# Two preparations of batch 2 issued ahead of theta of batch 1 instead of inside the attention of batch 1

## The chip, the core and the metric

The kernel runs on one core of a Trainium2 chip. The metric is the device time of one execution in microseconds (us), as the median of several runs. Engines: PE (TensorE) multiplies matrices, DVE (VectorE) and ACT (ScalarE) work elementwise, POOL (GpSimd) and SP (SyncE) mostly issue DMAs here. Each engine takes its instructions in order; semaphores make one wait for another.

## The reference

Two stages follow each other: a local attention with a few global keys, and a token-mixing layer with a phase. Inputs are q, k, v of 4 batches, 8 heads, 768 tokens, 64 channels, and four weights; the output is 4 x 768 x 512 in float32.

```python
scores = scale * q @ k.T - slope_h * dist        # kept: key < 8, or 0 <= query - key < 96
a = softmax(scores over the kept keys)
x = concat over heads of (a @ v)                 # 768 x 512
theta = x @ w_theta
y = w_tok_r @ (x * cos(theta)) + w_tok_i @ (x * sin(theta))
u = x + y
out = u + relu(u @ w_ch)
```

## The kernel before, in words

**Tiling.** 768 tokens are 6 tiles of 128. Heads go in 4 pairs, since two heads of 64 channels fill the 128 partitions. For a pair, `prep` (L249) copies q and k from the load buffer into qkn with the heads of a token side by side (`prep_copy`, L241, two DVE copies at L246), transposes qkn on PE (L261, 6 for q and 6 for k), copies the two results out as qT (DVE, L265) and kT (ACT, L267), and builds kG, the keys with the 8 global ones put in front of tiles 1 to 4 (`kglob`, L229, DVE at L235 and L237). `prep` of pair p also makes the copies of pair p+1. `score_mms` (L303) computes the kept blocks of scores of a pair in three chunks (L319) into a large PSUM buffer (`big`, 2 buffers of two banks); `score_exp` (L325) takes exp on ACT (L329) and multiplies by a table of biases on DVE (L338, L341). `values` (L362) multiplies by v (L381, also into a large PSUM buffer) and divides into x_sb (L386, L388). `xtrans` (L390) makes xT, the transpose of x_sb of a pair: in batch 1 by a DMA transpose issued by SP for pairs 0 to 2 (L392), by PE (L399) and ACT (L400) for pair 3.

**Mixing.** `theta` (L405) multiplies xT by w_theta (L422), over the four pairs dc = 0 to 3 in this order; `sines` (L427) takes cos and sin on ACT (L432, tile cs) and multiplies by x on DVE (L436, tile zri). `mix` (L441) does the token mixing of one output tile in three groups of four matmuls (L447) and adds x into u (L452). `utrans` (L456) transposes u (by PE at L465 for batch 0, by SP's DMA at L461 later), `chan` (L468) multiplies by w_ch (L475), adds on DVE (tile o_sb, L480) and stores by SP (L482). There are four small PSUM buffers (tile ps), which the transposes, the mix and chan share.

**Order of the work.** Batches overlap: while the mix of batch b runs on PE, the attention of batch b+1 is woven in. `weave` (L531) issues a list of main steps (mix, chan) and places side steps (the attention) between them by their weights. In batch 0 the four preps of batch 1 are side steps as well, ahead of the attention. Two preps of batch 2, for pairs 0 and 1, are in the list `ahead` (L652); `attention_steps` (L502) puts the first behind the fifth block of scores (L520) and the second behind the last one (L525), with a weight of 1536 each. Pairs 2 and 3 of batch 2 are prepared inside batch 2's own attention (L507, L519). Between two batches stands a boundary, the list `order` (L654): one remaining chan, the first four parts of theta, one more of the remaining steps (in batch 1 the utrans of the last tile of batch 0), the other two parts of theta, the remaining chans. In batch 1 `load_behind` (L496) stands ahead of it: a POOL copy (L497) reads a value of xT of pair 3, and behind it POOL issues the loads of the second half of batch 3's q and k (L82, 8 of 96 KB) and of its v (L88). The first half of batch 3's q and k is issued at the end of the weave of batch 0 (L679).

The part up to the middle of batch 0 is ordered by hand. From there a scheduler orders each engine's instructions, by the order of issue in the program and its own estimates; `behind` (L201) and `issue_after` keep given instructions behind an anchor. In `prep` the qkn copies stay behind the latest u (anchor "dve") and the transposes behind the latest mix matmul (anchor "pe").

POOL's loads run in the DMA queue q0 (software_dynamic), SP's transposes and stores in q1 (hardware_dynamic); both use the same 16 DMA engines.

Of the kernel before, what the change touches and what calls it, by code (L numbers as in the profile page):

```python
# [16 lines left out]
def kernel(  # L17
# [19 lines left out]
    NP = H // 2  # L37
# [18 lines left out]
    def ps_small(shape, dtype):  # L56
        return small.tile(shape, dtype, name="ps", tag="ps")
# [5 lines left out]
    def alloc_qk(b):  # L63
        loads[b] = [ld.tile([T, 2, H, NT, D], BF, name="qk"), None]
# [136 lines left out]
    def behind(eng):  # L201

        return tc.issue_after(anchor[eng]) if eng in anchor else nullcontext()
# [25 lines left out]
    def kglob(b, p, t0=0, t1=NT - 2, copy=nc.vector.tensor_copy):  # L229
        kT = qkT[(b, p)][1]  # L230
        if t0 == 0:
            qkT[(b, p)][2] = att.tile([T, NT - 2, T], BF, name="kG", bufs=6)
        kG = qkT[(b, p)][2][:, t0:t1]
        with behind("zri" if p else "dve") if b == B - 1 else nullcontext():
            copy(  # L235
                out=kG, in_=kT[:, (t0 + 1) * T:(t1 + 1) * T].rearrange("p (t n) -> p t n", t=t1 - t0))
            copy(out=kG[:, :, 0:NG], in_=kT[:, None, 0:NG].to_broadcast([T, t1 - t0, NG]))  # L237
# [3 lines left out]
    def prep_copy(b, p):  # L241
        qk = loads[b][0]
        qkn = qkns[b, p] = att.tile([T, NT, 2, 2, D], BF, name="qkn", bufs=2)
        with behind("dve"):
            for i_ in range(2):
                nc.vector.tensor_copy(  # L246
                    out=qkn[:, :, i_].rearrange("p t h d -> p h t d"), in_=qk[:, i_, 2 * p:2 * p + 2])

    def prep(b, p):  # L249
        if p == 0 or (b, p) == (2, NP // 2):  # L250
            prep_copy(b, p)
        if p + 1 < NP and (b, p) != (2, NP // 2 - 1):
            prep_copy(b, p + 1)
        qkn = qkns[b, p]
        qT = att.tile([T, S], BF, name="qT", bufs=6)
        kT = att.tile([T, S], BF, name="kT", bufs=6)
        for i_, dst in ((0, qT), (1, kT)):
            ps = ps_small([T, NT, T], BF)
            with behind("pe"):
                for t_ in range(NT):  # L260
                    nc.tensor.transpose(ps[:, t_, :], qkn[:, t_, i_].rearrange("p h d -> p (h d)"), ident)  # L261
            dst = dst.rearrange("p (n t) -> p n t", t=NT)
            src = ps.rearrange("p t n -> p n t")
            if i_ == 0:
                nc.vector.tensor_copy(out=dst, in_=src)  # L265
            else:
                nc.scalar.copy(out=dst, in_=src)  # L267

        qkT[(b, p)] = [qT, kT, None]
        kglob(b, p)  # L270

    def prep_dma(b, p):
        qk = loads[b][0]
        qkT[(b, p)] = [None, None, None]
        for i_ in (1, 0):
            to = qkT[(b, p)][i_] = att.tile([T, S], BF, name=("qT", "kT")[i_], bufs=6)
            with behind("sp"):
                nc.sync.dma_start_transpose(
                    out=to.rearrange("p (t s) -> p t s", t=NT),
                    in_=qk[:, i_, 2 * p:2 * p + 2].rearrange("p h t d -> p (h t d)"))  # L280
# [124 lines left out]
    def theta(b, c, j):  # L405
        last0 = [(j_, NC - 1) for j_ in range(2)]
        part = {0: [(0, dc) for dc in range(NC - 1)],
                1: [(1, dc) for dc in range(NC - 1)] + last0,
                2: [(j_, dc) for dc in range(NC - 1) for j_ in range(2)],
                3: last0,  # L410
                4: [(j_, dc) for dc in range(NC - 2) for j_ in range(2)],
                5: [(j_, NC - 2) for j_ in range(2)]}[j]
        if c == 0 and j in (0, 2, 4):
            zri[b] = moe.tile([T, 2, NT, DM], BF, name="zri", tag="zri", bufs=1)
        xT, xb = xT_sb[b], x_sb[b]
        last = c == NT // 2 - 1
        if j in (0, 2, 4):
            pss["th", c] = [ps_small([T, DM], FP) for _ in range(2)] if last else ps_big()
        pb = pss["th", c]
        st = lambda j_: slice((2 * c + j_) * T, (2 * c + j_ + 1) * T)  # L420
        for j_, dc in part:
            nc.tensor.matmul(pb[j_] if last else pb[:, j_, :], lhsT=xT[:, dc, st(j_)],  # L422
                             rhs=w_theta_bf[:, dc, :], start=(dc == 0), stop=(dc == NC - 1))
        if j == 1:
            sines(b, c)
# [15 lines left out]
    def mix(b, tt, g):  # L441
        if g == 0:
            pss["mix", tt] = ps_small([T, DM], FP)
        ps = pss["mix", tt]
        for wi in range(2):
            for st in (2 * g, 2 * g + 1):
                anchor["pe"] = nc.tensor.matmul(  # L447
                    ps, lhsT=w_tokT[wi][:, st, tt * T:(tt + 1) * T], rhs=zri[b][:, wi, st, :],
                    start=(st == 0 and wi == 0), stop=(st == NT - 1 and wi == 1)).ins
        if g == NT // 2 - 1:  # L450
            u_sb[b, tt] = moe.tile([T, DM], BF, name="u", bufs=6)
            anchor["dve"] = nc.vector.tensor_add(  # L452
                u_sb[b, tt].rearrange("p (g d) -> p g d", g=NP), x_sb[b][:, :, tt, :],
                ps.rearrange("p (g d) -> p g d", g=NP)).ins

    def utrans(b, tt):  # L456
        u = u_sb[b, tt]
        uT = moe.tile([T, NC, T], BF, name="uT", bufs=5)
        uTs[(b, tt)] = uT
        if (b or b) and (b, tt) != (B - 1, NT - 1):  # L460
            anchor["sp"] = nc.sync.dma_start_transpose(out=uT, in_=u).ins  # L461
            return
        ps = ps_small([T, NC, T], BF)
        for dc in range(NC):
            nc.tensor.transpose(ps[:, dc, :], u[:, dc * T:(dc + 1) * T], ident)  # L465
        nc.scalar.copy(out=uT, in_=ps)  # L466
# [22 lines left out]
    def load_all_v(b):  # L489
        alloc_v(b)  # L490
        load_v(b, 0, 8)
# [4 lines left out]
    def load_behind(b, tile):  # L496
        g = nc.gpsimd.tensor_copy(out=gate, in_=tile).ins  # L497
        with tc.issue_after(g):
            load_qk_tokens(b, H // 2, H // 2)
            load_all_v(b)  # L500
# [105 lines left out]
    p = NP - 1  # L606
# [39 lines left out]
    rest = []  # L646
    for b in range(B):
        nxt = b + 1 if b + 1 < B else None
        lag = 3
        th = [lambda c=c, j=j: theta(b, c, j) for c in range(NT // 2) for j in range(2)]  # L650
        pre = [lambda p=p: prep(1, p) for p in range(NP)] if b == 0 else []
        ahead = [[lambda p=p: prep(2, p) for p in range(NP // 2)], [lambda p=p: prep_dma(3, p) for p in range(1)],  # L652
                 [], []][b]
        order = rest[:1] + th[:4] + rest[1:2] + th[4:] + rest[2:] if b else []  # L654
        if b == 2:
            order[:0] = [lambda p=p: prep_dma(3, p) for p in range(1, NP)]
        if b == 1:
            order.insert(0, lambda: load_behind(3, xT_sb[1][0:1, NC - 1, 0:1]))
        for f in order:
            f()  # L660
        main = []
        for tt in range(0 if b else 2, NT):
            for g in range(NT // 2):
                if (b, tt) != (B - 1, NT - 1):
                    main.append((2048, lambda tt=tt, g=g: mix(b, tt, g)))
                if b == 0 and g == 1 and 4 <= tt + 2 < NT:
                    main.append((1536, lambda tt=tt: trans_w(tt + 2)))
                if tt >= lag and g == 0 and (b, tt) != (B - 1, NT - 1):
                    main.append((2048, lambda tt=tt: chan(b, tt - lag)))
                if b == 0 and g == 1:  # L670
                    main.append((512, lambda tt=tt: utrans(b, tt - 1)))
                if (b, tt, g) == (0, 2, 0):
                    main.append((512, lambda: utrans(0, 0)))
            if b and (b, tt) != (B - 1, NT - 1):
                main.append((0, lambda tt=tt: utrans(b, tt)))
        side = [(1536, f) for f in pre]
        if b == 0:
            side[:0] = [(0, lambda: load_all_v(2))]
            side.append((0, lambda: (alloc_qk(3), load_qk_tokens(3, 0, H // 2))))  # L679
        side += attention_steps(nxt, ahead) if nxt else []  # L680
        weave(main, side, 0.1 if b == 0 else 0.0, 0.9)
        rest = [lambda tt=tt, b=b: chan(b, tt) for tt in range(NT - lag, NT)]
        if b == 0:
            rest.insert(1, lambda b=b: utrans(b, NT - 1))
# [44 lines left out]
```

## Time and profile before

| what | value |
|---|---|
| runs | 172.28, 172.26, 171.69 us; median 172.26 |
| profiled execution | span 170.0 us; no time beside the span is recorded for it |
| PE busy | 158.1 us (93%) |
| DVE, ACT, POOL busy | 125.9 (74%), 102.1 (60%), 37.6 us (22%) |
| granted TensorE clock | 1.000 |
| chain that ended last | PE 56%, DMA 19%, DVE 16%, ACT 6% |
| 48.60 to 66.20 us (17.60) | PE busy 16.28, DVE 17.59, ACT 13.06 |
| 66.20 to 70.70 us (4.50) | PE busy 3.57, DVE 4.47, ACT 1.29 |
| 70.70 to 105.20 us (34.50) | PE busy 33.99, DVE 26.92, ACT 22.41 |

The profile is one execution, with times in us from the start of the span. The chain that ended last is followed back from the last instruction: each step is what released the next. The timeline lists instructions in order of time, like ones merged ("x3"); a bracket gives the idle time of the engine before them and what ended it. Busy time of PE is pipelined: matmuls of 512 columns are listed with 0.38 us each and follow each other every 0.22 us. The attention of batch 1 lies in about 43 to 68 us, the boundary between batch 0's mix and batch 1's theta at about 66 to 71 us.

### The profile page before, as it was taken

What the parts mean: (1) busy time and instruction counts of PE and PEld (TensorE: products, weight loads), DVE (VectorE), ACT (ScalarE), POOL (GpSimd) and SP (SyncE); (2) the same over time, 40 slices, a digit from 0 to 9 for tenths busy, and PEclk for the clock granted to TensorE, in tenths of its full rate; (3) what the DMA queues carried; (4) which work ended last, traced back from release to release, by engine and by line L of the source; (5) the groups of instructions that cost most, each with busy time, mean ns of one, the idle gap of its engine ahead of it and who ended that gap; (6) DMA issues with size and microseconds to landing.
All of it is one profiled execution on the core that took longest, in us unless ns stands there. A gap on an engine that the chain in (4) does not pass through costs nothing.

```text
span 170.0 us, 3773 instructions
## 1 busy us (share of the span) xinstructions
PE 158.1 (93%) x1544; PEld 85.4 (50%) x1566; DVE 125.9 (74%) x267; ACT 102.1 (60%) x131; POOL 37.6 (22%) x45
## 2 busy tenths in 40 slices
PE   7679999999989899799999999999999999999991
PEld 2346765657645555345555464444554644444440
DVE  6748877699989999957998787788776847614432
ACT  4698898995596585399954561899257309400010
POOL 8976319005262110696000000000000000000000
PEclk9999999999999999999999999999999999999999
DMA  4999999999999999999996879688135472233335
GB/s 147 205 171 179 210 207 205 203 209 180 152 203 189 188 153 182 127 163 149 184 112 57 165 167 130 132 152 241 35 77 139 113 169 80 109 61 93 93 93 185
DMA packets 73488, 25.53 MB, mean 150 GB/s; under 512 B 61568, under 2 KB 70528, under 8 KB 73472
## 3 DMA queue, kind: packets, MB, share of 16 engines
q0 software_dynamic: 45680, 12.45, 77.1%
q1 hardware_dynamic: 27376, 12.33, 32.9%
q10 hardware_dynamic: 416, 0.52, 0.9%
q8 instruction: 12, 0.20, 0.5%
q14 instruction: 4, 0.03, 0.0%
HBM read 25.69 MB, written 6.29 MB: 188 GB/s over the span
## 4 chain that ended last, share of the span: by engine, by line
PE 56%; DMA 19%; DVE 16%; ACT 6%; issue 2%; DVEq 0%
PE ps L447 26%; DMA vn<-in_v_dram 14%; PE ps L475 9%; PE pb L422 6%; PE pb L319 4%; PE pb L381 3%; PE ps L422 3%; DMA xT<-x_sb 3%; DMA qk<-in_k_dram 3%; DVE x_sb L388 3%; DVE e L338 2%; ACT e L329 2%; PE ps L215 1%; ACT cs L432 1%; DVE e L341 1%
## 5 line engine op out<-in xcount | busy, mean ns | idle before, releaser
L447 PE MATMUL ps<-zri,w_tokT 128*128 128x512 bf16 x272 | 67.5, 380 | 1.1 <-issue 0.3
L329 ACT ACTIVATE e<-pb 128x1024 bf16<-128x1024 f32 (+1 forms) x48 | 43.4, 954 | 17.4 <-PE pb L319 17.0
L447 PEld LDWEIGHTS <-w_tokT 128*128 128x128 bf16 x288 | 25.9, 98 | 27.8 <-DVE w_tokT L183 0.6
L452 DVE TENSOR_TENSOR u<-x_sb,ps 128x512 bf16<-128x512 bf16 x24 | 16.3, 680 | 11.7 <-PE ps L447 11.6
L475 PE MATMUL ps<-w_ch_bf,uT 128*128 128x512 bf16 (+1 forms) x96 | 24.1, 371 | 0.2
L436 DVE TENSOR_TENSOR zri<-x_sb,cs 128x1024 bf16<-128x1024 bf16 (+1 forms) x30 | 16.6, 581 | 6.3 <-ACT cs L432 6.1
L480 DVE SCALAR_TENSOR_TENSOR o_sb<-ps,u 128x512 f32<-128x512 f32 (+1 forms) x25 | 16.4, 663 | 4.1 <-PE ps L475 4.1
L319 PE MATMUL pb<-qT,kT 64*128 64x128 bf16 x224 | 15.4, 219 | 2.2 <-DVE qT L226 1.2
L338 DVE TENSOR_TENSOR e<-e,etab 128x1024 bf16<-128x1024 bf16 (+1 forms) x24 | 14.8, 618 | 3.1 <-ACT e L329 3.0
L432 ACT ACTIVATE cs<-pb,halfpi 128x1024 bf16<-128x1024 f32 x8 | 8.9, 1116 | 12.5 <-PE pb L422 12.4
L422 PE MATMUL pb<-w_theta_bf,xT 128*128 128x512 bf16 x62 | 15.0, 379 | 1.1 <-DMA xT<-x_sb 0.9
L319 PEld LDWEIGHTS <-kT 64*128 64x128 bf16 x224 | 8.9, 94 | 13.2 <-issue 11.3
L466 ACT COPY uT<-ps 128x512 bf16<-128x512 bf16 x7 | 4.2, 594 | 18.3 <-PE ps L465 18.1
L381 PEld LDWEIGHTS <-e 128*128 128x128 bf16 x352 | 13.0, 97 | 4.3 <-issue 1.6
L422 PEld LDWEIGHTS <-xT 128*128 128x128 bf16 x96 | 9.1, 98 | 11.8 <-DMA xT<-x_sb 1.9
L475 PEld LDWEIGHTS <-uT 128*128 128x128 bf16 x100 | 9.1, 98 | 9.6 <-ACT uT L466 0.8
L88 POOL DMA_DIRECT2D vn<-in_v_dram x5 | 9.6, 1915 | 12.7 <-DVE qkn L246 10.4
L319 PE MATMUL pb<-qT,kG 64*128 64x128 bf16 x128 | 11.5, 216 | 0.3 <-DVE kG L237 0.2
L388 DVE TENSOR_TENSOR x_sb<-pb,rec 128x768 bf16<-128x768 f32 x12 | 11.4, 953 | 0.3
L381 PE MATMUL pb<-vn,e 128*128 128x65 bf16 x168 | 9.9, 193 | 0.7 <-DVE x_sb L388 0.3
L341 DVE TENSOR_TENSOR e<-e,etab 128x1024 bf16<-128x1024 bf16 x12 | 8.2, 687 | 2.4 <-ACT e L329 2.4
L267 ACT COPY kT<-ps 128x768 bf16<-128x768 bf16 x8 | 6.4, 798 | 4.6 <-PE ps L261 4.4
(81 smaller groups left out, 209.4 us busy)
## 6 DMA issues: line engine op xcount, KB each, us to landing
out_dram<-o_sb SPq DMA_DIRECT2D x23, 256.0 KB, 2.3
vn<-in_v_dram POOLq DMA_DIRECT2D x3, 768.0 KB, 22.5
qk<-in_q_dram POOLq DMA_DIRECT2D x2, 768.0 KB, 21.1
qk<-in_k_dram POOLq DMA_DIRECT2D x2, 768.0 KB, 24.2
w_nat<-in_moe_w_tok_r_dram POOLq DMA_DIRECT2D x3, 384.0 KB, 15.7
w_nat<-in_moe_w_tok_i_dram POOLq DMA_DIRECT2D x3, 384.0 KB, 15.2
vn<-in_v_dram POOLq DMA_DIRECT2D x2, 384.0 KB, 10.2
qk<-in_q_dram POOLq DMA_DIRECT2D x8, 96.0 KB, 8.6
```

Source lines behind the costliest of these rows:

```text
L319: nc.tensor.matmul(pb[:, hh, o:o + T], lhsT=lhsT, rhs=qT[R, (own, nxt)[part]], start=bool(b), stop=bool(b) or (jt == NT - 1 or (j == 1 and ...
L329: ins = nc.scalar.activation(e_c, pb[:, :, 0:n], AF.Exp, scale=scale).ins
L338: nc.vector.tensor_mul(e_c, e_c, tab[:, :, s0:s0 + n // T].rearrange("p a s n -> p a (s n)"))
L381: nc.tensor.matmul(po4[:, head - h0, it - i0], lhsT=l_, rhs=r_, start=(i_ == 0), stop=(i_ == len(mms) - 1))
L388: nc.vector.tensor_mul(xv, po4[:, :, :, 0:D], rec.to_broadcast([T, n, nt, D]))
L422: nc.tensor.matmul(pb[j_] if last else pb[:, j_, :], lhsT=xT[:, dc, st(j_)], rhs=w_theta_bf[:, dc, :], start=(dc == 0), stop=(dc == NC - 1))
L432: nc.scalar.activation(o, p_, AF.Sin, **bias)
L436: anchor["zri"] = nc.vector.tensor_mul(zri[b][:, i_, 2 * c + j_:2 * c + j_ + n, :].rearrange("p j (g d) -> p j g d", g=NP), xb[:, :, 2 * c ...
L447: anchor["pe"] = nc.tensor.matmul(ps, lhsT=w_tokT[wi][:, st, tt * T:(tt + 1) * T], rhs=zri[b][:, wi, st, :], start=(st == 0 and wi == 0), ...
L452: anchor["dve"] = nc.vector.tensor_add(u_sb[b, tt].rearrange("p (g d) -> p g d", g=NP), x_sb[b][:, :, tt, :], ps.rearrange("p (g d) -> p g ...
L475: nc.tensor.matmul(ps_c, lhsT=uT[:, dc, :], rhs=w_ch_bf[:, dc, i_ * n:(i_ + 1) * n], start=(dc == 0), stop=(dc == NC - 1))
L480: nc.vector.scalar_tensor_tensor(o_sb[:, cols], in0=ps_c, scalar=0.0, in1=u[:, cols], op0=ALU.max, op1=ALU.add)
```

## The change

The two preps leave the list of `attention_steps`, which for batch 1 has no preps any more, and stand in the boundary of batch 1 between the first chan and theta. The boundaries of batches 2 and 3 stay as they were. `weave` of batch 0 has two side steps of 1536 less, so the other side steps get slightly different places between the main steps.

```diff
-        ahead = [[lambda p=p: prep(2, p) for p in range(NP // 2)], [lambda p=p: prep_dma(3, p) for p in range(1)],
+        ahead = [[], [lambda p=p: prep_dma(3, p) for p in range(1)],
                  [], []][b]
-        order = rest[:1] + th[:4] + rest[1:2] + th[4:] + rest[2:] if b else []
+        pr = [lambda p=p: prep(2, p) for p in range(NP // 2)]
+        order = rest[:1] + pr + th[:4] + rest[1:2] + th[4:] + rest[2:] if b == 1 else rest[:1] + th[:4] + rest[1:2] + th[4:] + rest[2:] if b else []
```

On each engine the number of instructions stays the same. In the new order of PE the 24 transposes of the two preps (L261) stand in one block: behind the last mix of batch 0, the transposes of x_sb of pair 3 (L399), of u (L465) and a chan (L475), and ahead of all 16 matmuls of the first four parts of theta (L422); in the order before, the first two of these 16 stood ahead of L399. On DVE the four qkn copies stand behind the last u of batch 0, followed by an o_sb, the two qT and the kG copies, and the vG copies of batch 2; zri comes after them. On ACT the two kT copies stand between the copy of xT of pair 3 with a copy of uT, and the first cs. The orders of SP and of POOL are unchanged.

## The prediction

> **What bounds the kernel now.** I read the page first: the busy table gives PE 93% of the span, and the chain that ended last is PE for 56%. But the 40 slices show DVE as full as PE in slices 12 to 15 (about 48 to 66 us), and this is where the change works. So I read the chain in order of time. It runs on DVE from 48.60 to 66.20, then in one DMA, then on PE:
>
> ```profile
> 61.38 0.87 DVE qT L265
> ...
> 64.50 0.81 DVE qT L265
> 65.31 0.86 DVE x_sb L388
> 66.17 0.03 DVE kG L235
> 66.20 4.49 DMA xT<-x_sb
> 70.69 0.05 issue
> 70.73 0.39 PE pb L422
> ```
>
> The reader is to see three links: DVE copies of the moved preparation (L265) stand ahead of the x_sb of pair 2 (L388, ends 66.17); that x_sb releases a DMA transpose (L392), which lands 4.49 us later; theta (L422) starts on that landing. From 70.73 to 105 nothing but PE is in the chain, and PE is busy 33.99 of the 34.50 us from 70.70 to 105.20.
>
> The second view is the timeline of SP, which issues the transposes of pairs 0, 1 and 2 of batch 1 (x2 merges the last two; they start at 59.54 and 66.20):
>
> ```profile
> 56.60 1.30 SPq L392 DMA_TRANSPOSE xT<-x_sb  x1
> 57.96 0.56 SPq L482 DMA_DIRECT2D out_dram<-o_sb  x1
> 59.54 7.88 SPq L392 DMA_TRANSPOSE xT<-x_sb  x2
> ```
>
> The view of tile xT gives what they took to land:
>
> ```profile
> DMA to landing us min/median/max: 4.5/7.6/8.4
> ```
>
> So pair 0 lands near 64.2, pair 1 near 67.9, pair 2 at 70.7. The third view, DMA queues by window, says why the first two are slow. In 57.9 to 61.1, after the issue of pair 0 has ended, there is only the software queue q0 (loads of POOL); in 61.1 to 63.3 both are served:
>
> ```profile
> q0 software_dynamic: 3552, 0.45, 316.5%
> ```
>
> ```profile
> q0 software_dynamic: 1080, 0.14, 108.5%
> q1 hardware_dynamic: 732, 0.19, 71.0%
> ```
>
> By the trace's packet records the 768 packets of 256 B of each transpose run 61.12 to 63.63, 64.44 to 66.92 and 67.38 to 70.24, with the 128 packets of an output store at 63.25 to 64.52 between the first two: q1 serves in the order of issue, about 2.5 us for each transpose while q0 is busy, and the last is 1.18 us behind its issue. Its landing is 0.45 us behind its last packet.
>
> **What leaves the attention.** Two prep calls: 4 qkn copies, 2 qT, 2 kG pairs on DVE, 2 kT on ACT, 24 PE transposes; they issue no DMA. In the chain up to x_sb of pair 2 DVE spends on them 0.21+0.54+0.27 (qkn), 0.87+0.81 (qT), 0.20+0.41 (kG) = 3.31 us. The new order on DVE also puts an o_sb (0.60) ahead of the vG copy that waits 0.73 us for vn (48.60), which fills that wait. If DVE stayed the bound, x_sb of pair 2 would end at 66.17-3.31-0.60 = 62.3. What is late next is the two large PSUM buffers, through which 12 score blocks and 4 values pass: with the same row durations the exp of the last block would end near 61.5, then e 0.47, rec 0.14, x_sb 0.86: 63.0. I take 63.0 (bounds 62.3 and, if half were lost, 64.2). Pair 3 follows by o_sb 0.60, rec 0.14, memset 0.1, x_sb 0.95: 64.8 in place of 68.19.
>
> **What arrives at the boundary.** On PE, after the mix and x_sb of pair 3: its 6 transposes 0.34 (to 65.2), u on DVE 0.6 (65.4), 4 transposes of u 0.22, chan 0.86 (66.5), then the 24 transposes at 0.67 per 12 = 1.34. The fourth group of them also waits for a small PSUM buffer that the o_sb behind the four qkn copies frees (65.4+4x0.31+0.60 = 67.2). They end at 67.6, and theta's first two matmuls, whose transposes landed long before, at 68.05. So 68.05 is the earliest start of the third, which needs pair 2. The kT copies on ACT (2x0.80) lie in its idle time ahead of cs, 2.16 us before 72.24. On DVE the moved work (4x0.33 qkn, 2x0.92 qT, 2x0.28 and 2x0.2 kG: 4.1 us) and what stood there (u 0.6, o_sb 0.6, vG 0.7+0.7, one qkn 0.35) end near 64.8+4.1+2.95 = 71.9; the first zri needs cs, 2.66 us after theta's third matmul starts (70.73 to 73.39), so about 73.0 at the forecast: 1.1 us in hand. Were that gone, each us late would delay only zri, which had 2.6 us between its second instruction's end (74.99) and the mix that reads it (77.59). I cost the moved work at nothing.
>
> **The transpose that ends last.** It is issued at 63.05, 3.15 us sooner, but it stands in q1 behind pair 1. What pair 0 waited for in 57.9 to 61.1 was q0, whose loads are not moved, so I keep 61.12 for its start although x_sb of pair 0 is 0.5 us earlier. Then pair 1 ends at 66.92 and pair 2 can start there, 0.46 sooner than 67.38. With 2.50 to 2.86 us of service and 0.45 to land it is there at 69.87 to 70.23. Two things pull. If the half us at pair 0 is won, 69.35. And the gate on POOL (L497), which in the kernel before opens at 69.65, behind the ACT copy of pair 3, now opens near 66.1, so the second half of batch 3's loads (96 KB each, 0.82 us of POOL each) follows the first half without the pause of q0 from 69.6 to 71. The last packets of pair 2, which had the engines alone (493 packets of q1 alone in 69.6 to 70.8), then share them: up to 0.6 us more. I take 70.3 for the landing: **0.4 us** gained, bounds 1.3 and -0.5. From there on the order on PE is the same up to the end, so the end moves by the same 0.4. Span 170.0 - 0.4 = 169.6; the page gives no time beside the span, and the median of the three runs is 172.26, 2.26 above it: 171.86, say **171.9**.
>
> [...]
>
> **Rivals.** A: pair 2 gets through faster (q1 is served early, or unhindered). For it: the third transpose landed in 4.49. Against it: the 7.6 and 8.4 of the others, at the time to which it moves. The gain runs from 1.3 to the PE bound, 70.73-68.05 = 2.7: 169.6 to 171.0.
> B, slower: the loads behind the gate that opens 3.5 us early hold q1 as the load in 57.9 to 61.1 held pair 0. If pair 2 is held 3.2 us from 66.92, it lands at 66.92+3.2+2.5+0.45 = 73.1, 2.4 us late: 174.6. It decides from a hold of 0.8 us on, since 69.87+0.82 is the landing of before. For it: that hold; against it: in 64.5 to 67 the same small loads let q1 have 799 packets beside 1540.
> C: DVE and PE do not get ahead as summed and the boundary's work delays theta. PE must be over 2.3 us later than 68.05 before it counts, or the 24 transposes cost their full 1.34: up to 173.6.
> That nothing moves is excluded: the new order has the 24 transposes in one block ahead of theta.
>
> **Numbers.** Forecast (within 0.5%, 0.86 us, about what a measurement can tell from no change): 0.48, its own range 171.2 to 172.9. A: 0.25, faster by over 0.5%. B: 0.17 and C: 0.10, slower. The range for 8 in 10 takes in the bounds and half of A and of B's and C's near side: 170.6 to 173.2.
>
> **What would show it.** In the profile after: DVE no longer in the chain just ahead of xT; the third L392 issued at 62.3 to 64.2; a landing time of 7 us in place of 4.5; PE idle ahead of L422 of 1.5 to 2.5 us on the DMA; the chain after it unchanged. It is wrong if PE reaches theta later than the landing, if the landing is before 69.3 (A), or after 71.2 (B).

## The result and the profile after

The changed kernel takes 174.06 us (median of 6; 173.62 to 175.73) beside 171.92 us (171.69 to 172.28, 6) for the kernel before on the same chip: ratio 1.0134, 95% interval 1.0103 to 1.0164. It is slower by 2.1 us; 171.9 had been forecast, with 173.2 as the upper end. Some executions of several kernels here lie more than 1.5% above its fastest; ratios and intervals leave these out, medians take them in unless the text says otherwise. The profiled execution took 173.81 us, with a span of 171.8 us (before: 170.0) and a mean granted clock of 0.990 (before: 1.000).

The chain of the changed kernel in order of time (start, us, what; "..." marks lines left out, here and below):

```profile
62.19 0.96 DVE x_sb L388
63.15 0.03 DVE o_sb L480
63.18 7.79 DMA xT<-x_sb
70.97 0.04 issue
71.01 4.83 PE pb L422 x14
75.85 0.22 PE ps L465 x4
...
79.52 0.51 PE ps L447 x2
```

The x_sb of pair 2 ends at 63.15, 3.0 us sooner, as summed (63.0). But the transpose now takes 7.79 us in place of 4.49, so theta's third matmul starts 0.28 us *later*, at 71.01. And theta's remaining 14 matmuls take 4.83 us; in the kernel before they took 3.2 us (70.73 to 73.93). The mix of batch 1 starts at 79.52 (before: 77.75), and 1.8 us is also what the span has grown by. The same part of the chain before:

```profile
70.73 0.39 PE pb L422
71.12 0.05 issue
71.17 2.75 PE pb L422 x12
...
77.75 0.86 PE ps L447 x4
```

The view of tile xT gives the landings of the three transposes:

```profile
DMA to landing us min/median/max: 7.7/7.8/8.1
```

The third is issued at 63.18 and lands, like the other two, after more than 7 us. By the packet records the three are served in 60.41 to 62.85, 63.56 to 65.64 and 67.48 to 70.55: behind the second there is a hold of 1.84 us, in which the transposes' queue stands nearly still. The DMA queues in this hold (packets, MB, share of 16 engines, over 100% where an engine has several packets under way):

```profile
q0 software_dynamic: 2170, 0.27, 235.6%
q1 hardware_dynamic: 8, 0.00, 0.6%
```

Only q0, the loads, moves. Theta's slow matmuls are explained by the page's row of the granted clock, and by the busy times of two stretches, from the end of the first two theta matmuls to the landing, and theta behind it (us; PE, PEld, DVE, ACT, POOL busy; clock, DMA share, GB/s):

```profile
PEclk9999999999999999789999999999999999999999
```

```profile
68.30:71.00 2.70, 0.01 (x1) 0.00 (x0) 2.70 (x8) 0.45 (x1) 2.70 (x4) 0.99 1.39 186
71.00:75.85 4.85, 4.84 (x17) 1.94 (x18) 1.55 (x4) 2.03 (x2) 4.65 (x4) 0.65 2.20 182
```

PE waits 2.70 us in one piece, and then the clock stands at 0.65 over theta. By the clock records it is halved from 70.95 for 3.41 us. This reading looked complete, and the first experiments were built on it. It was half of the cause. The other half does not appear in this chain, but in DVE's and POOL's timelines of the same execution (L436 makes zri, L88 loads v):

```profile
74.94 0.69 DVE L436 TENSOR_TENSOR zri<-x_sb,cs 128x1024 bf16<-128x1024 bf16 x1 [3.30 <-ACT cs L432]
75.55 0.72 DVE L246 COPY qkn<-qk 128x768 bf16<-128x768 bf16 x1
76.19 0.67 DVE L436 TENSOR_TENSOR zri<-x_sb,cs 128x1024 bf16<-128x1024 bf16 x1
76.79 0.61 DVE L246 COPY qkn<-qk 128x768 bf16<-128x768 bf16 x2
77.32 1.31 DVE L436 TENSOR_TENSOR zri<-x_sb,cs 128x1024 bf16<-128x1024 bf16 x2
78.70 0.69 DVE L480 SCALAR_TENSOR_TENSOR o_sb<-ps,u 128x512 f32<-128x512 f32 x1
```

```profile
73.90 2.22 POOL L88 DMA_DIRECT2D vn<-in_v_dram  x1 [0.20 <-PE pb L422]
```

Three qkn copies (for pairs 2 and 3 of batch 2) stand between the zri. In the kernel before they were done at 70.80 to 72.08, ahead of the first zri at 73.39:

```profile
70.80 1.28 DVE L246 COPY qkn<-qk 128x768 bf16<-128x768 bf16 x3
71.07 0.84 POOL L82 DMA_DIRECT2D qk<-in_k_dram  x1
73.39 0.69 DVE L436 TENSOR_TENSOR zri<-x_sb,cs 128x1024 bf16<-128x1024 bf16 x1 [1.30 <-ACT cs L432]
76.77 2.27 POOL L88 DMA_DIRECT2D vn<-in_v_dram  x1
```

In the changed kernel the order is zri, copy, zri, two copies, two zri. The first of these three copies lasts 0.72 us in place of 0.35 and ends at 76.27, just behind POOL's issue of the v load (73.90 to 76.12; before: from 76.77, since the gate L497 opened at 69.65 and not, as here, at 66.35). The o_sb that frees the small PSUM buffer for the mix ends at 79.39, the mix starts on PE's own chain at 79.52. So in this execution two late chains arrive within 0.13 us of each other, and the chain view shows only the later one.

### The profile page after: what moved, and what is told of

Its sections match the earlier page's. It is cut to its first block, busy times and chain, and to the rows that moved or that the text cites. A ratio compares the mean times of both kernels' runs of the same rounds, so it can differ in the third digit from the quotient of the medians.

```text
span 171.8 us, 3795 instructions
## 1 busy us (share of the span) xinstructions
PE 159.9 (93%) x1566; PEld 85.0 (49%) x1566; DVE 126.8 (74%) x267; ACT 102.4 (60%) x131; POOL 38.0 (22%) x45
## 4 chain that ended last, share of the span: by engine, by line
PE 68%; DVE 14%; ACT 8%; DMA 7%; issue 1%; DVEq 0%; ACTq 0%
PE ps L447 31%; PE ps L475 9%; PE pb L422 8%; PE pb L319 5%; ACT e L329 5%; DMA xT<-x_sb 5%; PE ps L422 4%; PE pb L381 4%; DMA qk<-in_k_dram 2%; DVE qT L265 2%; DVE e L338 1%; DVE x_sb L388 1%; ACT cs L432 1%; DVE kG L235 1%; PE pbw L179 1%; DVE e L341 1%
## 5 line engine op out<-in xcount | busy, mean ns | idle before, releaser
L447 PE MATMUL ps<-zri,w_tokT 128*128 128x512 bf16 x288 | 70.3, 380 | 0.0
L447 PEld LDWEIGHTS <-w_tokT 128*128 128x128 bf16 x288 | 25.8, 98 | 27.5 <-DVE w_tokT L183 0.6
L475 PE MATMUL ps<-w_ch_bf,uT 128*128 128x512 bf16 (+1 forms) x100 | 24.3, 371 | 0.0
L436 DVE TENSOR_TENSOR zri<-x_sb,cs 128x1024 bf16<-128x1024 bf16 (+1 forms) x30 | 16.5, 580 | 7.4 <-ACT cs L432 7.2
L422 PE MATMUL pb<-w_theta_bf,xT 128*128 128x512 bf16 x64 | 16.6, 410 | 2.7 <-DMA xT<-x_sb 2.7
L422 PEld LDWEIGHTS <-xT 128*128 128x128 bf16 x96 | 9.4, 102 | 14.1 <-DMA xT<-x_sb 3.2
L475 PEld LDWEIGHTS <-uT 128*128 128x128 bf16 x100 | 9.1, 98 | 9.5 <-ACT uT L466 0.6
L88 POOL DMA_DIRECT2D vn<-in_v_dram x5 | 9.5, 1905 | 13.8 <-DVE qkn L246 11.1
L82 POOL DMA_DIRECT2D qk<-in_q_dram x8 | 7.0, 870 | 8.2 <-DMA qk<-in_k_dram 3.8
```

The costliest lines, as they stand in the source:

```text
L436: anchor["zri"] = nc.vector.tensor_mul(zri[b][:, i_, 2 * c + j_:2 * c + j_ + n, :].rearrange("p j (g d) -> p j g d", g=NP), xb[:, :, 2 * c ...
L447: anchor["pe"] = nc.tensor.matmul(ps, lhsT=w_tokT[wi][:, st, tt * T:(tt + 1) * T], rhs=zri[b][:, wi, st, :], start=(st == 0 and wi == 0), ...
L475: nc.tensor.matmul(ps_c, lhsT=uT[:, dc, :], rhs=w_ch_bf[:, dc, i_ * n:(i_ + 1) * n], start=(dc == 0), stop=(dc == NC - 1))
```

## Experiments

Line numbers shift by up to 8 in edited kernels. "Before" is the kernel before on the same chip.

**Does the gate that opens early hold the third transpose?** (the prediction's rival B)

```diff
-            order.insert(0, lambda: load_behind(3, xT_sb[1][0:1, NC - 1, 0:1]))
+            order.insert(0, lambda: load_behind(3, xT_sb[1][0:1, NC - 2, 0:1]))
```

> The changed kernel with the gate of batch 3's second half of loads reading xT of pair 2, so that they start behind its landing and not 3.3 us sooner. Theory (clock): these loads delay the third transpose only by the share of the engines that they take in its last microsecond; it lands 0.2 to 0.5 us sooner, near 70.6, PE still waits over 2.2 us, the clock still drops, 173.4 to 174.0. Rival 2 (the early gate is what makes the kernel slower): it lands near 69.5, the wait falls to 1.2 us, no drop of the clock, 171.0 to 171.6.

Measured: 173.63 us, ratio 1.0071 (1.0037 to 1.0105). The gate now waits for the third transpose itself, so none of these loads runs before 72, and yet the hold is 2.5 us (packets 64.12 to 66.29, then but for 9 only from 68.78) and the landing takes 8.37 us. For about 0.9 us of this hold all queues together move less than 30 GB/s. The early gate does not make the hold. The forecast drop of the clock is not in this profile: PE waits 3.22 us and theta runs at full clock (3.19 us). Three more things in it became clear only later: the v load is issued behind 79, the longest qkn copy between the zri is 0.45 us, and the mix follows theta's third matmul by 7.03 us (72.16 to 79.19) as in the kernel before (70.73 to 77.75).

**Does the wait cost the clock?** Dummy matmuls, which do work that is thrown away, fill PE's wait in the changed kernel (e_fill, and e_fill2 and e_fill12 of the same kernel on other chips; e_again is the changed kernel unedited on the chip of e_fill2):

```diff
         for j_, dc in part:
+            if (b, c, j, dc) == (1, 0, 0, 2):
+                for _ in range(12):
+                    nc.tensor.matmul(pb[:, 1, :], lhsT=xT[:, 1, st(0)], rhs=w_theta_bf[:, 1, :],
+                                     start=True, stop=True)
```

> The changed kernel with 12 extra matmuls of 512 columns between the second and the third matmul of theta of batch 1, in the 2.70 us in which PE waits for the transpose of pair 2; their result is overwritten by the group that starts in the same buffer. Theory (clock): the loss is the clock that is granted at half for 3.41 us because PE stood idle before theta. Then the clock stays at 1.000, the 14 matmuls of theta behind the wait take 3.0 us and not 4.83, and the time is 172.0 to 172.4, as before the change. Rival 1 (the moved work itself, 1.34 us of transposes in front of theta, and the 0.28 us later landing): the extra matmuls lie in a wait and change nothing, or add to it: 174.0 or more.

> The changed kernel with 12 extra matmuls in the wait ahead of theta's third matmul, once more beside the unedited one. Their result is overwritten. Theory (clock): theta's 14 matmuls take 3.0 us, and it is 0.7 to 1.5 us faster than the unedited one of this call, still 0.3 to 1.2 us above before for the later landing. Rival 1: as slow as the unedited one.

> The changed kernel once more, without an edit, beside the runs of this call. Theory (clock): PE again stands idle over 2 us ahead of theta's third matmul, a stretch of 3.41 us at half clock falls at theta, and the time is 1.0 to 1.5% above that of before. Rival 1 (the moved work itself): the same time, but also in executions that keep the full clock through theta.

Measured: e_fill 173.39 us, 1.0066 (1.0043 to 1.0090); e_fill2 173.36 us, 1.0040 (1.0003 to 1.0078); e_again 174.55 us, 1.0111 (1.0047 to 1.0176). In PE's timeline theta's 14 matmuls take 4.88 us in e_again and 3.19 in e_fill2; these are e_again's:

```profile
68.21 0.38 PE L422 MATMUL pb<-w_theta_bf,xT 128*128 128x512 bf16 x1
70.84 4.88 PE L422 MATMUL pb<-w_theta_bf,xT 128*128 128x512 bf16 x14 [2.25 <-DMA xT<-x_sb]
```

In the medians the clock theory had its gain, 1.2 us between e_again and e_fill2 on one chip, but it is only 0.5 us (173.84 and 173.35) when the longest execution of each is left out, and the intervals overlap. Above all, in the edited kernels the scheduler had also put the three qkn copies back ahead of the first zri. These runs therefore changed two things at once; that showed only in a later profile which the clock could not explain.

The same question without the move, in the kernel before, where the qkn copies keep their places (in e_idle2 alone one o_sb and one zri, behind the first four zri, change places): extra DMA transposes of pair 2 into a tile that is no longer read delay the third one, without and with 12 dummies (e_idle and e_idle_fill: one extra; e_idle2 and e_idle_fill2: two, as below).

```diff
+        if (b, p) == (1, 2):
+            for spare in (distS, dist):
+                nc.sync.dma_start_transpose(
+                    out=spare, in_=x_sb[b][:, p].rearrange("p t d -> p (t d)"))
```

> The kernel before, without the move, with one more DMA transpose of x_sb of pair 2 (into a table that is no longer read) in SP's queue ahead of the one that theta waits for. So theta waits longer, by 1.3 to 2.8 us, and PE stands idle 2.2 to 3.7 us. Theory (clock): an idle stretch of this length costs a half-clock stretch of 3.41 us at theta with no move at all, so the loss is the longer wait plus 1.5 to 1.8 us: 174.5 to 176.5. Rival 1: the loss is the longer wait alone: 173.3 to 175.0, with theta's matmuls at full clock.

> The run with the extra transpose, and 12 extra matmuls, whose result is overwritten, in the wait that it makes. Theory (clock): the wait stays, the half clock goes: 1.5 to 1.8 us faster than the same without the extra matmuls. Rival 1: no faster than without them.

> The kernel before, without the move, with two more DMA transposes of x_sb of pair 2 (into two tables that are no longer read) ahead of the one that theta waits for. One of them made theta wait 0.94 us longer and PE idle 1.94 us in one piece, without a drop of the clock. Theory (clock): with two of them PE stands idle 2.7 to 4 us, as with the move, and in most executions a half-clock stretch of 3.41 us falls at theta: the longer wait, 1.8 to 2.8 us, plus 0.9 to 1.8 us: 175.0 to 176.8, with the profile's clock under 0.7 in theta. Rival 1: the longer wait alone, 174.0 to 175.0, theta's 14 matmuls in 3.0 to 3.2 us.

> The run with two more transposes, and 12 extra matmuls in the wait that they make; the result of the matmuls is overwritten. Theory (clock): theta's 14 matmuls in 3.0 to 3.2 us and the longer wait alone, 174.0 to 175.0, that is 0.9 to 1.8 us less than without the extra matmuls. Rival 1: no less than without them.

Measured: one extra gives a wait of 1.94 us, no drop at theta, 172.77 us, 1.0049 (1.0018 to 1.0080), and with dummies 173.22 us, 1.0067 (1.0035 to 1.0099): nothing to cure. Two extra give 175.15 us (174.38 without the longest of four), 1.0142 (1.0077 to 1.0206), with dummies 173.33 us, 1.0065 (1.0044 to 1.0085), though theta's third matmul starts at the same time in both profiles (72.72 and 72.64). PE's timeline of e_idle2:

```profile
72.72 2.75 PE L426 MATMUL pb<-w_theta_bf,xT 128*128 128x512 bf16 x12 [2.42 <-DMA xT<-x_sb]
```

This profiled execution had full clock and a span of 171.6 us; two others had mean clocks of 0.979 and 0.989 and spans of 172.6 and 173.9 us. With dummies all four lie in 171.0 to 171.8. So with no qkn copy moved, waits of this length went with about 1 us more (174.38 beside 173.33); from three and four executions, with intervals that overlap, this is an indication. That the clock does it is shown for theta in the profiles of the changed kernel and of e_again. For e_idle2 the mean clocks only suggest it: beside it the kernel before has 0.970 to 0.989 in five of ten executions, with spans of 171.1 us at most.

**Does the move cost anything if PE does not wait?** Pair 2 is transposed by PE and ACT in both kernels (`xtrans`):

```diff
-        if b > 2 or (b and p < NP - 1):
+        if b > 2 or (b and p < NP - 1 - (b == 1)):
```

> The kernel before with xT of pair 2 of batch 1 made by PE and ACT, as in the run beside it, so that the two differ by the move alone, with the wait for the third transpose gone in both. Theory: theta can start when x_sb of pair 3 is there, near 69.3, for 170.7 to 171.5, that is 1 to 1.5 us slower than with the move. Rival 1: faster than with the move by 1.3 us or more.

> The changed kernel with xT of pair 2 of batch 1 made by PE and ACT, like pair 3, in place of SP's DMA transpose: 6 more transposes on PE (0.34 us), one more copy on ACT (0.8 us). Theory (the wait for the third transpose hides what the move gains and then costs the clock): theta starts near 68.3 with no long wait ahead of it, the clock stays at 1.000, and the kernel is faster than both: 169.3 to 170.5. Rival 1 (the moved work itself): the copies on DVE and the transposes on PE stand ahead of theta as before, little is won: 172.5 to 174.

Measured: without the move 171.54 us, 0.9946 (0.9921 to 0.9971), faster than both kernels; with it 172.74 us, 1.0010 (0.9975 to 1.0045). The wait is gone in both; without the move theta starts at 68.89 and runs through:

```profile
68.89 3.62 PE L422 MATMUL pb<-w_theta_bf,xT 128*128 128x512 bf16 x16
```

With it, DVE and then PE wait (DVE, POOL and PE in the timeline of an execution of 174.40 us, from which I read only order and single durations):

```profile
73.92 2.31 POOL L88 DMA_DIRECT2D vn<-in_v_dram  x1
74.64 1.73 DVE L246 COPY qkn<-qk 128x768 bf16<-128x768 bf16 x1
76.30 0.67 DVE L436 TENSOR_TENSOR zri<-x_sb,cs 128x1024 bf16<-128x1024 bf16 x1
...
77.89 0.81 PE L447 MATMUL ps<-zri,w_tokT 128*128 128x512 bf16 x3 [2.14 <-DVE o_sb L480]
```

The qkn copy beside the v issue lasts 1.73 us and the mix waits 2.14 us for an o_sb behind it. Behind the wait for this o_sb the clock is lower as well: by the clock records it is halved from 79.11 for 3.41 us, over the mix (in the chain four L447 take 1.02 us at 77.89 and 1.82 at 79.68). I had first put the 1.2 us between the two kernels down to the amount of DVE work moved; these lines point to one copy. How much of the 1.2 us it makes, this one execution does not show.

The preparation set behind the first four parts of theta, with pair 2 by PE (`order = rest[:1] + th[:4] + pr + ...` and the edit above):

> The changed kernel with xT of pair 2 made by PE and ACT, and with the two preps behind the first four parts of theta instead of ahead of them. In the run with the preps ahead, DVE reached the first zri at 72.3 behind 7 us of copies, which took the place of the wait for the transpose. Theory: with the copies behind, theta starts near 67.0 and zri follows cs, and the moved work lies in the idle time of DVE between the zri: 169.5 to 171.0, faster than the kernel before with the same edit (171.5). Rival 1 (the moved work costs itself wherever it stands in the boundary): 171.5 to 172.8.

Measured: 172.62 us, 1.0030 (1.0001 to 1.0059). Its chain:

```profile
67.04 0.65 PE pb L422 x3
...
68.80 3.95 ACT cs L432 x4
72.75 0.70 ACT kT L267
...
73.49 1.89 PE ps L422 x8
```

Theta runs from 67.04 without a wait for pair 2, but its last third then waits for a small PSUM buffer that a kT copy frees behind four cs on ACT. The early start is lost to a new wait.

**Is the hold a fetch of instructions?** In the profiles a 16 KB transfer on an instruction queue (q8) stands at the beginning of the hold: at 65.6 (0.97 us) in the changed kernel, 66.0 in e_gate; in the kernel before at 67.8, inside the third transpose. 76 tiny matmuls at the kernel's start shift PE's program:

```diff
     warm(6)
+    ps_pad = ps_small([T, 512], FP)
+    for _ in range(76):
+        nc.tensor.matmul(ps_pad[0:16, 0:16], lhsT=zero[:, 0:16], rhs=zero[:, 0:16], start=True, stop=True)
```

> The changed kernel with 76 extra matmuls of 16 columns (152 instructions of PE) in the first microseconds, where PE waits for the first load, so that every later instruction of PE stands 152 places further on in its program. Theory (the third transpose is held by the 16 KB fetch of instructions on queue q8, which in the runs so far lies between the second and the third transpose): the fetch moves away from 65 to 68 us, the third transpose follows the second within 0.3 us and lands near 69.2, the wait ahead of theta falls to 1.0 us, the clock stays at full: 171.0 to 172.0. Rival 3 (the third is held by the software queue's loads, whatever the fetch does): the gap of 1.0 to 1.8 us stays, 173.4 to 174.3. The extra matmuls may themselves cost up to 1 us at the start; the profile tells it apart.

Measured: 175.62 us, 1.0157 (1.0088 to 1.0226). The fetches move to 62.1 and 72.0, and the hold is gone: the second and third transpose follow each other without a gap (66.09 to 71.64). But the two take 5.55 us, the landing 6.99, and the padding delays everything by about 2 us. That the hold goes with the fetch is a correlation, and that curing it saves time is not shown. The other profiles make it weaker still. In the seven of the changed kernel, with or without dummies (e_again, e_again2, the four e_fill and e_fill_order), the fetch starts at 65.5 to 66.6 and q1 pauses behind it for only 0.67 to 0.81 us, mostly inside the second transpose; in three of them a second pause of 0.33 to 0.73 us follows. Yet the third transpose ends at 69.85 to 71.14 in these, beside 70.55 in the changed kernel with its hold of 1.84. Its packets take 2.62 to 3.64 us there and 3.07 here, up to 0.8 us more than the 2.86 of the kernel before. So the hold of 1.84 us is one execution's; the late landing is common to all. At full clock (theta's 14 in 3.20 us) this profile also runs through a qkn copy, of 1.93 us, ahead of its mix.

**Wait or order: two by two.** The unedited kernel once more (e_again2), with 4 dummies (e_fill4), and half of the change (e_half: pair 0 stays in the attention, `ahead = [[lambda: prep(2, 0)], ...`, `pr = [lambda: prep(2, 1)]`):

> The changed kernel unedited, as the yardstick for the other three on this chip. Both theories: 173.9 to 174.6 with the kernel before at 172.2. [...]

> The changed kernel with only 4 dummy matmuls there (about 0.9 us of PE work, so that 1.4 to 1.9 us of the wait is left). Clock theory: with an idle time below the 1.94 us that left the clock full in an earlier run there is no drop at theta, so the time is that of the 12 dummies, 172.9 to 173.5. If any wait of over a microsecond can halve the clock, it lies half way to the changed kernel, near 174. Landing theory: the time of the changed kernel.

> The changed kernel with 12 dummy matmuls between theta's second and third part, once more, beside the changed kernel on the same chip. Clock theory (PE's one-piece wait ahead of theta halves the granted clock over theta): 172.9 to 173.5, at least 1.0 us below the changed kernel of the same chip, theta's 14 matmuls 3.0 to 3.2 us. Landing theory (the loss is the late third transpose and the moved work, the clock is chance): within 0.3 us of the changed kernel.

> Half of the change: only the preparation of pair 1 stands at the boundary, that of pair 0 stays inside the attention. The third x_sb then ends near 64.8 (half of 3.3 us sooner than 66.17), the third transpose follows the second without a gap and lands at 70.3 to 70.9. Clock theory: the work ahead of theta on PE ends later than in the changed kernel (x_sb of pair 3 near 66.6 in place of 64.9), so the wait is 1.3 to 2.0 us, the clock stays full, and the time is 171.6 to 172.8. Landing theory: 173.0 to 173.8, half way between the two kernels, since half of the work is moved.

Measured: e_again2 174.36 us, 1.0107 (1.0057 to 1.0156); e_fill4 172.33 us, 1.0016 (0.9986 to 1.0045); e_fill12 173.00 us, 1.0041 (1.0006 to 1.0077); e_half 173.83 us, 1.0111 (1.0055 to 1.0166). e_half lies at the edge of the landing theory's range, but that theory had forecast the time of the unedited kernel for e_fill4 and misses it by 2 us. The surprise is e_again2's profile: PE waits 2.49 us, theta runs at *full* clock (3.19 us), and yet the span is 172.3 us. Its chain behind theta, and DVE beside POOL in the timeline:

```profile
71.69 1.48 PE pb L422 x6
...
74.34 0.69 DVE zri L436
75.03 1.94 DVE qkn L246
76.97 0.24 DVE zri L436
...
79.23 0.69 DVE o_sb L480
79.92 0.04 issue
79.96 1.02 PE ps L447 x4
```

```profile
74.55 2.24 POOL L88 DMA_DIRECT2D vn<-in_v_dram  x1
74.95 2.02 DVE L246 COPY qkn<-qk 128x768 bf16<-128x768 bf16 x1
76.89 0.67 DVE L436 TENSOR_TENSOR zri<-x_sb,cs 128x1024 bf16<-128x1024 bf16 x1
```

From theta's third matmul to the mix it takes 8.27 us, 1.25 more than in the kernel before (7.02), without any loss of clock: the qkn copy lasts from 74.95 to 76.97, the v issue from 74.55 to 76.79. In e_fill4, whose order has the copies ahead of zri, the same distance is 7.01 us (71.11 to 78.12). The 12 dummies, 2.59 us of PE work, are themselves in the chain of e_fill12, up to theta's third matmul at 71.06, so they may be a dearer cure than 4; the intervals of the two overlap. e_half has the old order too; its profile shows full clock and no long copy, but begins with 6.8 us at half clock, and why its other executions (spans up to 173.4 us) are as slow as those of the whole change is not settled.

So the two effects had to be parted. e_order puts the copies ahead of zri without dummies (the vG copies of batch 2 and the copies are issued at the boundary; every other engine keeps the changed kernel's order). e_fill_order has the 4 dummies and holds DVE to the changed kernel's order:

```diff
+        pr += [lambda: vglob(2, 0, H)] + [lambda p=p: prep_copy(2, p) for p in range(NP // 2, NP)]
         order = rest[:1] + pr + th[:4] + ...
```

```diff
-        with behind("dve"):
-            for i_ in range(2):
+        for i_ in range(2):
+            with behind("z%d" % (p - 2)) if (b, p, i_) in ((2, 2, 1), (2, 3, 0), (2, 3, 1)) else behind("dve"):
...
+                if (b, c) == (1, 0):
+                    anchor["z%d" % i_] = anchor["zri"]
```

> The changed kernel with one thing put back on DVE: the last three of the four qkn copies of pairs 2 and 3 of batch 2 stand ahead of the first zri of batch 1's theta, as in the kernel before, in place of between the zri; every other engine's order is that of the changed kernel, and there are no dummy matmuls. Clock theory (the loss is theta at half clock): no help, 174.0 to 174.6 with the kernel before at 172.2. Order theory (the loss is a qkn copy that stands ahead of the second zri and lasts until POOL's v load issue ends, about 75 to 77 us): 172.2 to 172.7, no qkn copy over 0.6 us in the profile. Both, each hiding the other: between, 172.8 to 173.8, low where the clock stays full.

> The changed kernel with 4 dummy matmuls between theta's second and third matmul, but with DVE's order held to that of the changed kernel (the dummies alone had moved the qkn copies back ahead of zri). Clock theory: the time of the 4 dummies alone, 172.2 to 172.6 with the kernel before at 172.2. Order theory: 173.4 to 174.4, with a qkn copy of 1 to 2 us between two zri in the profile and DVE in the chain behind theta. Both, each hiding the other: 173.3 to 174.0 with theta's 14 matmuls at 3.0 to 3.2 us.

Measured, medians in us (ratios to before, which had 172.22 beside e_again2 and e_fill4 and, on another chip, 172.17 beside e_order and e_fill_order):

| | DVE's order of the changed kernel | qkn copies ahead of zri, as before |
|---|---|---|
| PE waits | 174.36, 1.0107 (1.0057 to 1.0156) | e_order 172.96, 1.0034 (1.0002 to 1.0067) |
| 4 dummies | e_fill_order 173.32, 1.0045 (1.0011 to 1.0078) | e_fill4 172.33, 1.0016 (0.9986 to 1.0045) |

The order alone is worth 1.4 us, the filled wait alone 1.0, both 2.0. The theory of both hits the two new runs (172.8 to 173.8 and 173.3 to 174.0). The clock theory misses by over a microsecond on e_order; the order theory misses both by 0.1 to 0.3, which is within what the medians can tell. Only the corner with both cures is clear of e_again2 by its interval; beside the first measurement of the changed kernel (1.0103 to 1.0164) all three are. Two causes that only hid one another would make the single gains add up to less than 2.0, and here they add up to 2.4: the table shows that each cure helps, not how the two share the loss. That there are two rests on the profiles as well: theta at half clock in two of three of the unedited changed kernel, a long copy between the zri (0.72, 1.44 and 2.02 us) in all three. The chain of e_fill_order runs, at full clock, through the copy:

```profile
70.34 1.48 PE pb L426 x6
...
73.96 0.65 DVE zri L440
74.60 1.26 DVE qkn L246
...
77.56 0.69 DVE o_sb L486
78.25 0.04 issue
78.29 0.81 PE ps L453 x3
```

Theta's third matmul starts here at 70.34, the earliest of all with this transpose by DMA, and 7.95 us pass up to the mix. In e_order they are 7.03:

```profile
71.64 3.19 PE pb L422 x14
...
78.67 0.86 PE ps L447 x4
```

This execution of e_order had lost its time at the start (half clock from 7.8 to 18.0 us, x_sb of pair 2 at 66.1), and PE waits only 0.37 us for the transpose in it; so it shows the cured order without a long wait beside it. The two executions of e_order with a mean clock of 1.0 have spans of 169.6 and 169.8 us, where those of the kernel before at 1.0 beside it lie in 169.7 to 170.3.

## Why the prediction was wrong

**What leaves the attention**: right. x_sb of pair 2 ended at 63.15 (63.0 forecast), that of pair 3 at 64.9 (64.8).

**What arrives at the boundary, on PE**: right. Theta's first two matmuls, put at 67.6 behind the 24 transposes, start at 67.72; PE then waits for the transpose, not the other way round.

**The transpose that ends last**: the mechanism was right (issued early, stuck in q1 behind pair 1, over 7 us to land, PE idle), the term "pair 1 ends at 66.92 and pair 2 can start there" was mis-sized. Pair 1 ended sooner (65.64), but pair 2 started 1.84 us behind it, and its packets took 3.07 us in place of 2.50 to 2.86. Landing 70.97 in place of 70.3, inside the bound of -0.5; but the terms given for that bound, 70.23 and 0.6, only reach 70.83, or -0.1. Not rival B: e_gate has the hold without the early loads. In the hold the two queues did not share evenly: 8 packets of q1 beside 2170 of q0.

**"From there on the order on PE is the same up to the end, so the end moves by the same 0.4"**: this step failed first. The order on PE was the same; its clock was not. The prediction had forecast "PE idle ahead of L422 of 1.5 to 2.5 us" and given it no price. Measured, theta behind 2.70 us of idle time took 1.6 us longer (4.83 against 3.2) in the profiled execution, and filling the wait is worth 1.0 us in the median (e_again2 to e_fill_order). The length of the wait alone does not tell when this happens: theta ran at half clock behind 2.25 us in e_again (4.88 us) and at full clock behind 2.49 us in e_again2 (3.19 us).

**"I cost the moved work at nothing"**: this step failed second. The sum of DVE's work was right (the end of the work ahead of zri was put at 71.9; the last vG copy ends at 71.64), but it counted "one qkn" of what stood there: the other three copies had moved behind the first zri, in the new order of DVE. The prediction saw 2.6 us in hand for the later zri; three copies of 0.35 would have fitted. What it missed is the neighbour: the gate opens 3.3 us earlier, so POOL's v issue moves from 76.77 to 73.90, onto these copies, and the one that starts inside it, at 75.55, ended 0.15 us behind it (76.27 against 76.12); in five other profiles a qkn copy did the same (e_again, e_again2, e_fill_order, e_pe_after, e_pad). The kernel before already had a sign of it, in the three qkn copies beside POOL's short issues at 70.80: these issues were no longer than elsewhere (0.84 and 0.83 against 0.82 to 0.87), but the copies were. The three took 1.28 us in that row, beside 0.88 in e_fill4; the third lasted 0.66 us and ended 0.17 us behind POOL's issue (71.91). The issue that mattered later (L88, 2.2 us) is only longer. The place was also not rival C's: DVE was late not ahead of theta but behind it.

Both failures have one root: the work ahead of theta was done 3 us sooner, but the third transpose was not. The slack only moved, and each place where it went (PE's wait, POOL's early issue) had a price that was put at zero. One more term: the 2.26 us added to the span came from a median of three; with the median of six, 171.92, it is 1.9, and the forecast gain of 0.4 stands for 171.5. What stays open: what makes the third transpose late, behind which waits the clock falls, e_half's time, and whether the move gains anything over 171.54 us once pair 2 is transposed by PE *and* the qkn copies stand ahead of zri; the last was not tried. No version with the move was faster than the kernel before in the median; the fastest kernel of this study is the one before with pair 2 transposed by PE.

## What to carry to other kernels

Follow every instruction that changes its neighbours, not only the ones that are moved: here the loss came from three copies that the diff does not name and from a load that a gate let go early. A forecast wait ahead of a dense stretch of PE can be a cost in itself: here the matmuls behind waits of 2.14, 2.25 and 2.70 us ran at half clock, behind waits of 2.42, 2.49 and 3.22 us at full clock, and behind those of 1.94 us or less that were looked at (e_idle, e_pad, e_fill4, e_fill_order, kernel before) at full clock too. When an experiment recovers the loss, compare the order on every engine before believing its cause; two chains that end within 0.13 us of each other hide one another in the chain view, and undoing each alone and both together is the way to part them.

## What the runs showed of the hardware

**A qkn copy beside POOL's v issue ended behind it.** The qkn copy (0.34 to 0.35 us alone) that started 0.4 us or more into the v issue (L88) ended 0.14 to 0.18 us behind that issue in all six profiles that have the pair, whatever its own start: it lasted 0.72 us in the changed kernel, 1.44 (e_again), 2.02 (e_again2), 1.66 (e_fill_order), 1.73 (e_pe_after) and 1.93 us (e_pad). In e_again another copy, which started 0.16 us into the issue, kept 0.35 us. Copies beside POOL's shorter issues (L82) did the same: 0.66 us in the kernel before, ended 0.17 us behind the issue. In e_gate, with the v issue out of the way, the longest of the three was 0.45 us. The zri beside the same issue, with two inputs, kept 0.67 to 0.69 us. In the other direction POOL's 96 KB issue lasted 2.01 us beside a row of DVE copies in e_fill4 (71.06), against 0.83 to 0.92 for the issues around it.

**Behind some waits the clock was halved for 3.41 us.** PE idle in one piece ahead of theta and the clock behind it: 2.70 us, half (changed kernel, mean 0.65 over 71.00 to 75.85); 2.25, half (e_again, mean 0.65 over 70.84 to 75.70); 2.49, full (e_again2); 3.22, full (e_gate); 2.42, full (e_idle2); 1.94 and less, full (e_idle, e_pad, e_fill4, e_fill_order, kernel before). A third drop, over the mix, came behind 2.14 us (e_pe_after). In the clock records the changes lie 19, 1 and 29 times 3.413 us apart in the changed kernel and 48 times in the kernel before. In the 3.41 us ahead of the three drops PE was busy for 0.77, 1.21 and 1.27 us (23 to 37%); in e_gate it was busy for 0.18 of the 3.40 us from 68.90 to 72.30 (5%), and the clock stayed full. The clock also fell in the third of the 40 slices of seven profiles (the row of the clock has 5 or 6 there), behind a slice in which PE was busy for 4 or 5 tenths; six others, with 3 to 5 tenths in it, kept it. So neither the length of a wait nor the busy share ahead of it parts the drops from the rest here; what does was not shown. The wait of 2.70 us went with 1.6 us more over theta, those of 2.49 and 3.22 us with none.

**The queue of the transposes stood nearly still while another went on.** In the hold of the changed kernel q1 had 8 packets in 1.84 us while q0 went on at 148 GB/s. A 16 KB fetch on q8 starts at its beginning, and pauses of q1 of 0.67 to 0.81 us follow the fetch in seven other profiles. Where the fetch fell inside the third transpose (67.8 in the kernel before, 68.5 in e_order), or at 62.2 and 72.0 (e_pad), no such pause followed, so the fetch alone does not make it.
